# One PSUM tile of eight banks, and one reader instruction for both heads' scores

## The chip, the cores and the metric

The kernel runs on one NeuronCore of a Trainium2 chip. Its engines work side by side, each through its own list of instructions in order: TensorE (PE in the profile, with its weight loads as PEld), VectorE (DVE), ScalarE (ACT), GpSimd (POOL) and SyncE (SP, which here issues most of the DMAs). They wait for one another by semaphores. Matrix products go into PSUM, a memory of eight banks; a bank holds 512 fp32 numbers for each of 128 partitions, which is one score block here. VectorE and ScalarE read the results from there.

The metric is the time of one execution on the device in microseconds (us); less is better.

## The reference, cut to what matters

The model mixes a self-attention of 32 heads with a channel MLP, token by token, by a gate. All data are fp32.

```
B, S, D = 1, 2048, 576;  H = 32;  Dh = D // H = 18;  F = 4608
g = sigmoid((x * gate_w).sum(-1, keepdims=True))

q, k, v = split(x @ wqkv)                         # 32 heads of 18
scores = einsum("bhqd,bhkd->bhqk", q, k) * Dh ** -0.5
p = softmax(scores, axis=-1)
a = einsum("bhqk,bhkd->bhqd", p, v) -> (S, D) @ wo

y = layernorm(x)
h = gelu(y @ w1 + b1)                             # tanh form
b = h @ w2 + b2
out = g * a + (1 - g) * b
```

## The kernel before

**Attention.** The heads are taken in 16 pairs, and the 2,048 queries in two halves, which makes 32 units. TensorE has 128 rows; head 0 of a pair stands in rows 0 to 63 and head 1 in rows 64 to 127, so that the two heads' score products of L230 or L275, which use 54 to 56 rows each, can run at the same time. The softmax needs each query's largest score before the exponentials, and the kernel computes the scores twice for that:

- *Maxima rounds* (`s1_round`, L220): 128 queries against 512 keys. For each head one matmul (L230) writes a PSUM bank, and one VectorE `tensor_reduce` (L232) reads it and writes the 128 maxima of that block into `M4`. A unit has 32 rounds, there are 1,024 in all. They run ahead of the unit that uses them. When a unit is complete, `s1_finish` (L234) makes the maxima into two extra rows of the query operand.
- *Exponential rounds* (`s2`, L267): 128 keys against 512 queries, with the maxima subtracted by the extra rows. For each head one matmul (L275) writes a bank and one ScalarE `activation` with Exp (L278) reads it into a tile `p`, which has room for both heads. These, too, are 1,024 rounds.
- *Products with V* (`pv`, L282): matmuls of L293 multiply `p` by V, into one accumulator bank for a unit (16 chunks of 128 keys), which `o_store` (L300) copies out and sends to DRAM. They come in groups, 16 matmuls for two chunks or 24 for three.

**The MLP as filler.** The MLP's work is cut into small pieces by a generator (`mlp`, L342) and put between the rounds. Its first product, `h_pair` (L465, matmuls of L494), writes two banks for two chunks of the hidden layer, 54 matmuls for a pair; VectorE and ScalarE read these (L514, L515), and the GELU goes on over ScalarE and GpSimd. Its second product, `out_pair` (L552, matmuls of L582), writes two banks too, 48 matmuls for 128 tokens, and VectorE adds them to a running sum (L599). Before the attention loop stands the phase that makes Q, K and V (L886 to L918, with transposes and layer norm), with some maxima rounds between; after it the product with `wo` (`out_proj`, L1041, L1229).

**The order.** The kernel sets `manual_schedule`, so that each engine executes in the order in which the program calls it; the framework adds the semaphores. In the loop at L1280 each step is a key chunk of a unit: an exponential round, filler, a maxima round, at every second or third step a group of L293, then again an exponential round, filler, a maxima round, filler. The lengths of filler pieces and the due times of deferred work (`defer`, `run_due`) are written in as estimated nanoseconds.

**PSUM banks before.** Each use has its own pool of one-bank tiles: `ps_s1` (three banks) and `ps_o` (one) throughout, `ps_a` (four) before the loop, and in its place `ps_s2` (two) and `ps_w` (two) in the loop. `score_bank` (L121) gives a score matmul its bank. It is called once for each head, and counts through five banks in the loop (three of `ps_s1`, two of `ps_s2`) and four before it (three of `ps_s1`, and `ps_o`). A matmul that is to write a bank waits until the last reader of what stood in it is done.

Of the kernel before, what the change touches and what calls it, by code (L numbers as in the profile page):

```python
# [8 lines left out]
F32 = mybir.dt.float32  # L9
F32R = mybir.dt.float32r  # L10
AF = mybir.ActivationFunctionType
ALU = mybir.AluOpType
# [4 lines left out]
P = 128  # L17
# [16 lines left out]
GC0 = 1.0 / 0.044715  # L34
LN_EPS = 1e-5
HALF = S // 2
NS1 = 3
LEAD = 4
FILL = 1250.0
SLOT = 950.0  # L40
# [29 lines left out]
def gated_mix_kernel(ctx: ExitStack, tc: tile.TileContext, x, wqkv, wo, w1, b1, w2, b2, gate_w, out):  # L70
# [32 lines left out]
    pp = ctx.enter_context(tc.tile_pool(name="pp", bufs=2))  # L103
    hp = ctx.enter_context(tc.tile_pool(name="hp", bufs=6))
    asm = ctx.enter_context(tc.tile_pool(name="asm", bufs=2))
    ps_s1 = ctx.enter_context(tc.tile_pool(name="ps_s1", bufs=NS1, space=PSUM))
    ps_o = ctx.enter_context(tc.tile_pool(name="ps_o", bufs=1, space=PSUM))
    QA = [att.tile([P, HALF], F32R, name=f"qa{i}") for i in range(3)]
    KA = [att.tile([P, S], F32R, name=f"ka{i}") for i in range(2)]
    VT = [att.tile([P, NT, VW], F32, name=f"vt{i}") for i in range(2)]  # L110
# [2 lines left out]
    V0 = att.tile([P, NT, VW], F32, name="v0")  # L113
    oe = att.tile([P, TB], F32, name="oe")

    def psum(pool):
        return pool.tile([P, TB], F32, name="ps")

    ring = [0]

    def score_bank():  # L121

        ring[0] += 1
        if not looped[0]:
            return psum(ps_s1 if ring[0] % (NS1 + 1) < NS1 else ps_o)
        return psum(ps_s1 if ring[0] % (NS1 + 2) < NS1 else ps_s2)

    def big_tile():
        return yp.tile([P, 9, TB], F32R, name="big")
# [62 lines left out]
    def unit(u):  # L192
        return UNITS[u]
# [26 lines left out]
    def s1_round(u, r):  # L220


        t, kb = (r % 8, r // 8) if u in (0, NU - 3) else divmod(r, 4)
        if r == 0:
            M4[u] = asm.tile([P, 2, 8, 4], F32, name="m4")
        qa, ka = QA[u % 3], KA[unit(u)[0] % 2]
        for h in range(2):
            r0 = 64 * h
            ps = score_bank()
            nc.tensor.matmul(ps, qa[r0:r0 + 54, t * P:(t + 1) * P], ka[r0:r0 + 54, kb * TB:(kb + 1) * TB],  # L230
                             start=True, stop=True)
            nc.vector.tensor_reduce(M4[u][:, h, t, kb:kb + 1], ps, axis=AX.X, op=ALU.max)  # L232

    def s1_finish(u):  # L234

# [28 lines left out]
    def p_of(n):  # L264
        return RING[n % 4 if n < TWOS else (n - TWOS) % 3]

    def s2(u, kc, qb):  # L267
        qa, ka = QA[u % 3], KA[unit(u)[0] % 2]
        n = u * NT + kc
        if n < 2 and qb == 0:  # L270
            RING.insert(n, pp.tile([P, 2, 2, TB], F32, name="p"))
        ps = [score_bank() for _ in range(2)]
        for h in range(2):
            r0 = 64 * h
            nc.tensor.matmul(ps[h], ka[r0:r0 + 56, kc * P:(kc + 1) * P], qa[r0:r0 + 56, qb * TB:(qb + 1) * TB],  # L275
                             start=True, stop=True)
        for h in range(2):
            nc.scalar.activation(p_of(n)[:, qb, h], ps[h], AF.Exp, scale=SCALE)  # L278

    OB = {}  # L280

    def pv(n, m):  # L282

        u, kc = divmod(n, NT)
        if kc == 0:
            OB[u] = psum(ps_o)
        v = v_of(unit(u)[0])
        for c in range(n, n + m):
            for qb in range(2):
                for h in range(2):  # L290
                    r = 32 * (2 * h + qb)
                    k = c % NT
                    nc.tensor.matmul(OB[u][r:r + 32, :], v[:, k, 19 * h:19 * h + 32], p_of(c)[:, qb, h, :],  # L293
                                     start=(k == 0), stop=(k == NT - 1))
        if kc + m == NT:
            o_store(u, OB.pop(u))
# [45 lines left out]
    def mlp():  # L342
# [122 lines left out]
        def h_pair(q, last, inner=False):  # L465
# [5 lines left out]
                yield 0  # L471
            wt = ready(W1, q)
            del W1[q]
            ps = [psum(ps_w) for _ in range(2)]
            if q == 0:
                slots = [(w_, 0, c) for c in range(9) for w_ in (0, 1)] + [(0, 1, c) for c in range(9)]
            else:
# [74 lines left out]
        def out_pair(i, t, acc):  # L552

            tb, g = seq[i]
            tok = slice(t * P, (t + 1) * P)
            cs = [slice(nn * ND, (nn + 1) * ND) for nn in range(2)]
            ps = [psum(ps_w) for _ in range(2)]
            skip.clear()
            if piece[0]:
                ends = cuts(24, GAPS - piece[0]) | {12}  # L560
            elif rounds:
                ends = set(TURNS)
                skip.add(3)
            else:
                ends = set(TAIL)
                skip.update((2, 3))
            k = 0
            ends_at = []
            for turn in range(2):
                if turn == 1:  # L570
                    nc.tensor.wait_ge(swap, swaps[0])
                for j in ORDER:
                    while (i, j) not in HT:
                        cut[0] = 3
                        yield 0
                    hh, hl = HT[i, j]
                    w_ = ready(W2, (i * (G // 2) + j // 2, j % 2))
                    for h_, p_ in ((hh, 0), (hh, 1), (hl, 0)):
                        for h in (0, 1) if turn == 0 else (1, 0):
                            r = slice(64 * h, 64 * h + 64)  # L580
                            nn = h ^ turn
                            mm = nc.tensor.matmul(ps[nn][:, :ND], h_[r, tok], w_[p_][r, cs[nn]],  # L582
                                                  start=(k == 0), stop=(k == 6 * G - 1))
                            if k == 3 * G - 1:
                                ends_at.append(mm)
                        k += 1
                        if k == 3 * G:

                            seen = nc.scalar.sem_inc(swap, 1)
                            swaps[0] += 1  # L590
                            for mm in ends_at:
                                behind_of(seen, mm)
                        if k < 6 * G:
                            if k in ends:
                                cut[0] = 1
                            yield 131
            for nn in range(2):
                dst = acc[:, t, cs[nn]]
                nc.vector.scalar_tensor_tensor(dst, ps[nn][:, :ND], 0.5, b2b[:, cs[nn]] if g == 0 else dst,  # L599
                                               op0=ALU.mult, op1=ALU.add)  # L600
            if g == NG - 1:
                tt = tb * 4 + t
                nc.gpsimd.tensor_scalar(acc[:, t, :], acc[:, t, :], gate1[:, tt:tt + 1], 1.0, op0=ALU.mult, op1=ALU.mult)

                def store():
                    nc.sync.dma_start(b_scr[tt * P:(tt + 1) * P, :], acc[:, t, :])
                    kept[0] += 1
                defer(12 if tb < NB - 1 else 4, store)
            cut[0] = 2
            yield 131  # L610
# [106 lines left out]
    with ExitStack() as a:  # L717
        wpool = a.enter_context(tc.tile_pool(name="a_w", bufs=1, side="right"))
        sm = a.enter_context(tc.tile_pool(name="a_sm", bufs=2, side="right"))
        ps_a = a.enter_context(tc.tile_pool(name="ps_a", bufs=4, space=PSUM))  # L720

        qkstack = ExitStack()
        wqk = qkstack.enter_context(tc.tile_pool(name="a_wqk", bufs=1))
# [41 lines left out]
                eng.tensor_tensor(lo[:, cs], raw[:, cs], hi[:, cs].bitcast(F32), op=ALU.subtract)  # L765

        def transposed(tb, c):
            ps = psum(ps_a)
            for t in range(4):
                nc.tensor.transpose(ps[:, t * P:(t + 1) * P], x_view(tb)[:, t, c * P:(c + 1) * P], ident)  # L770
            return ps
# [63 lines left out]

        def stat_rows(tb):

            ps = psum(ps_a)
            nc.tensor.transpose(ps[:, :P], stp, ident)
            nc.scalar.activation(strow, ps[:8, :P], AF.Copy)  # L840
            nc.sync.dma_start(st_scr[tb], strow)
# [44 lines left out]
        def qk_group(tb, mt):  # L886
            big = xT[tb]
            wh, wl = W_QK
            ms = slice(mt * P, (mt + 1) * P)
            ps = psum(ps_a)  # L890
            k = 0
            for c in range(4):
                for w_, s_ in ((wh, c), (wh, 4 + c), (wl, c)):
# [12 lines left out]
        def v_group(tb, t, n, between=None):  # L906
# [1 line left out]
            tok = slice(t * P, (t + 1) * P)  # L908
            cs = slice(n * ND, (n + 1) * ND)
            wh, wl = W_V  # L910
            ps = psum(ps_a)
            k = 0
            for c in range(4):
                for s_, w_ in ((c, wh), (c, wl), (4 + c, wh)):
# [36 lines left out]
        for tb in range(NB):  # L951
            work = [(qk_group, (tb, mt)) for mt in (range(9) if tb < 2 else (4, 0, 1, 2, 3, 5, 6, 7, 8))] + [(v_group, (tb, t, n)) for t in range(4) for n in range(2)]
            for g, (fn, args) in enumerate(work):
# [35 lines left out]
                if tb == NB - 1:  # L989
                    if g == 0:  # L990
                        next(stream[0])
                    if g == 1:
                        load_k(0, 3 * TB, S)
                    if g == 2:
                        load_q(1)
                        next(stream[0])
                    if g == 9:
                        qkstack.close()
                        wp1 = mstack.enter_context(tc.tile_pool(name="m_w1", bufs=3))
                        wp2 = mstack.enter_context(tc.tile_pool(name="m_w2", bufs=4))  # L1000
                        next(stream[0])
                    if g == 7:
                        ps = psum(ps_a)
                        nc.tensor.transpose(ps[:, :NFC], b1r, ident[:NFC, :NFC])
                        nc.vector.tensor_copy(b1t, ps[:, :NFC])
                if tb == 1 and g == 5:
# [19 lines left out]
                    run_due()  # L1026


    ps_s2 = ctx.enter_context(tc.tile_pool(name="ps_s2", bufs=2, space=PSUM))
    ps_w = ctx.enter_context(tc.tile_pool(name="ps_w", bufs=2, space=PSUM))  # L1030
    cw = ctx.enter_context(tc.tile_pool(name="c_w", bufs=1, side="right"))
    ring2 = cw.tile([P, 2, 2, TB], F32, name="ring2")
    rstack = ExitStack()
# [7 lines left out]
    def out_proj():  # L1041
# [165 lines left out]
        for b in range(NB):  # L1207
# [6 lines left out]
            for t in range(4):  # L1214
# [5 lines left out]
                res = io.tile([P, D], F32, name="res", bufs=6)  # L1220
                for n in range(2):
                    cs = slice(n * ND, (n + 1) * ND)
                    ps = psum(ps_w)
                    k = 0
                    for c in range(5):
                        while done[b] <= c:
# [120 lines left out]
```

## Time and profile before

| | |
|---|---|
| time, median of 3 runs | 2213.79 us (2212.21 to 2215.25) |
| the profiled execution | 2212.78 us |
| its span, first to last instruction | 2211.0 us |
| TensorE busy | 2197.4 us, 99% of the span |
| VectorE busy | 1647.9 us, 75% |
| ScalarE busy | 1425.9 us, 64% |
| GpSimd busy | 1003.7 us, 45% |
| L232, maxima | 2,048 instructions, 684 ns each |
| L278, exponentials | 2,048 instructions, 596 to 597 ns each |

How to read the rows that follow. A group of instructions is told as line, engine, operation, output<-input, and shapes; behind the count (x) stand the busy time in us and the mean of one in ns, and behind the bar the engine's idle time just before these instructions, with whom it waited for. In a row of the timeline the first number is the start in us from the span's beginning, the second the length, and the last number behind an x how many instructions in a row are merged; [0.30 <-ACT p L278] says that the engine had been idle for 0.30 us and that this instruction released it. In a row of the busy time by stage the stage and its length come first, then busy us and count for PE, PEld, DVE, ACT and POOL (or for PE and PEld alone, where a single line's instructions are asked for), the granted TensorE clock (1.00 is full), the share of the DMA engines and GB/s. Matmuls overlap in TensorE's pipeline, so that their lengths add up to more than the time that they take.

### The profile page before, as it was taken

The page shows a single profiled execution, that of the slowest core. Times are in us where ns is not written, and L with a number is a line of the kernel's source. Part 1 is how long each engine was busy: PE and PEld are TensorE (multiplying, and loading weights), DVE is VectorE, ACT ScalarE, POOL GpSimd, SP SyncE. Part 2 cuts the span into 40 slices and gives each one's busy share as a digit, 9 for nine tenths or more (in the row PEclk, how much of TensorE's full clock was granted, in tenths as well). Part 3 has the DMA queues.
Part 4 walks back from the last instruction along what each step waited for, and adds up shares of the span by engine and source line. Part 5 has one row for each costly group of instructions (what it writes and reads, how often), then busy time and mean ns, then how long its engine had stood idle before and what let it go on. Part 6 is the DMA issues. An engine that isn't in the chain of part 4 may idle for free.

```text
span 2211.0 us, 51479 instructions
## 1 busy us (share of the span) xinstructions
PE 2197.4 (99%) x20496; PEld 1578.5 (71%) x20496; DVE 1647.9 (75%) x2888; ACT 1425.9 (64%) x2623; POOL 1003.7 (45%) x1000
## 2 busy tenths in 40 slices
PE   8999999999999999999999999999999999999999
PEld 7877666676667776677766777767776777776668
DVE  6675777777778778777777777777776777777734
ACT  4333777777776666666666666666665666666672
POOL 4331766666664444444444444444444444444800
PEclk9999999999999999999999999999999999999999
DMA  8867655444464623333354424233464333242265
GB/s 263 276 217 224 199 175 156 154 160 151 152 198 139 197 101 123 121 124 105 115 173 150 138 81 136 101 125 101 125 176 146 109 113 120 98 153 101 77 224 169
DMA packets 171640, 329.74 MB, mean 149 GB/s; under 512 B 65314, under 2 KB 91614, under 8 KB 160672
## 3 DMA queue, kind: packets, MB, share of 16 engines
q1 hardware_dynamic: 168850, 322.67, 45.2%
q8 instruction: 161, 2.64, 0.5%
q10 hardware_dynamic: 2454, 3.75, 0.5%
q14 instruction: 79, 0.65, 0.1%
q0 software_dynamic: 96, 0.03, 0.0%
HBM read 234.00 MB, written 96.69 MB: 150 GB/s over the span
## 4 chain that ended last, share of the span: by engine, by line
PE 95%; DVE 2%; DMA 1%; issue 0%; POOL 0%; ACT 0%; SPq 0%; DVEq 0%; ACTq 0%; POOLq 0%
PE ps L293 21%; PE ps L582 21%; PE ps L494 20%; PE ps L275 13%; PE ps L230 11%; PE ps L894 3%; PE ps L1229 3%; PE ps L915 2%; DVE m L232 1%; PE ps L770 0%; DMA p<-in_A_wqkv_dram 0%; DMA big<-y_scr 0%; PE ps L897 0%; PE ps L896 0%; DVE st L857 0%
## 5 line engine op out<-in xcount | busy, mean ns | idle before, releaser
L232 DVE TENSOR_REDUCE m<-ps 128x1 f32<-128x512 f32 x2048 | 1311.3, 684 | 390.3 <-PE ps L230 380.3
L278 ACT ACTIVATE p<-ps 128x512 f32<-128x512 f32 x1048 | 568.3, 597 | 301.7 <-PE ps L275 299.3
L278 ACT ACTIVATE ring<-ps 128x512 f32<-128x512 f32 x1000 | 543.2, 596 | 294.9 <-PE ps L275 291.8
L494 PE MATMUL ps<-big,w 64*128 64x512 f32 x3708 | 569.4, 393 | 0.2 <-issue 0.2
L183 POOL TENSOR_SCALAR zz<-zz 128x512 f32<-128x512 f32 x288 | 178.1, 618 | 743.3 <-ACT zz L547 686.1
L582 PE MATMUL ps<-w,hh 64*128 64x288 f32 x4352 | 477.4, 294 | 1.5 <-DVE x L599 1.5
L275 PE MATMUL ps<-qa,ka 56*128 56x512 f32 x2048 | 448.6, 420 | 1.1 <-ACT p L278 0.3
L582 PEld LDWEIGHTS ps<-w,hh 64*128 64x128 f32 x4352 | 417.2, 186 | 32.5 <-DVE x L599 6.2
L230 PE MATMUL ps<-ka,qa 54*128 54x512 f32 x2048 | 425.6, 397 | 0.1
L494 PEld LDWEIGHTS ps<-big,w 64*128 64x128 f32 x3708 | 369.8, 187 | 66.1 <-issue 0.5
L183 POOL TENSOR_TENSOR zz<-zz,z 128x512 f32<-128x512 f32 x288 | 371.4, 1290 | 24.0
L275 PEld LDWEIGHTS ps<-qa,ka 56*128 56x128 f32 x2048 | 204.4, 184 | 226.3 <-DVE m L232 174.7
L582 PE MATMUL ps<-w,hl 64*128 64x288 f32 x2176 | 339.3, 292 | 0.8 <-POOL hl L183 0.8
L293 PE MATMUL ps<-p,vt 128*32 128x512 f32 x1968 | 239.1, 598 | 0.0
L230 PEld LDWEIGHTS ps<-ka,qa 54*128 54x128 f32 x2048 | 213.4, 184 | 22.6 <-DVE m L232 2.6
L293 PE MATMUL ps<-ring,vt 128*32 128x512 f32 x1872 | 227.6, 598 | 0.0
L582 PEld LDWEIGHTS ps<-w,hl 64*128 64x128 f32 x2176 | 222.2, 184 | 1.2 <-POOL hl L183 1.1
L183 POOL TENSOR_TENSOR hl<-zz,hh 128x512 fp32r<-128x512 f32 x136 | 176.6, 1299 | 11.4
L183 POOL TENSOR_TENSOR w<-x,w 128x576 fp32r<-128x576 f32 (+1 forms) x54 | 98.8, 1842 | 164.1 <-ACT w L398 158.4
L293 PEld LDWEIGHTS ps<-p,vt 128*32 128x32 f32 x1968 | 52.5, 109 | 111.8 <-issue 102.7
L293 PEld LDWEIGHTS ps<-ring,vt 128*32 128x32 f32 x1872 | 49.8, 109 | 106.4 <-issue 106.4
L599 DVE SCALAR_TENSOR_TENSOR x<-ps,x 128x288 f32<-128x288 f32 x256 | 103.6, 446 | 8.8 <-PE ps L582 8.4
(121 smaller groups left out, 1538.2 us busy)
## 6 DMA issues: line engine op xcount, KB each, us to landing
w<-w_scr SPq DMA_DIRECT2D x54, 1152.0 KB
w<-w_scr SPq DMA_DIRECT2D x108, 576.0 KB
x<-in_B_w_dram SPq DMA_DIRECT2D x72, 288.0 KB
w_scr<-w SPq DMA_DIRECT2D x18, 1152.0 KB
w_scr<-w SPq DMA_DIRECT2D x36, 576.0 KB
qa<-qk_scr SPq DMA_DIRECT2D x192, 72.0 KB
ka<-qk_scr SPq DMA_DIRECT2D x84, 144.0 KB
qk_scr<-hh SPq DMA_DIRECT2D x36, 256.0 KB
```

The source lines that it names most:

```text
L183: fn(*args, **kw)
L230: nc.tensor.matmul(ps, qa[r0:r0 + 54, t * P:(t + 1) * P], ka[r0:r0 + 54, kb * TB:(kb + 1) * TB], start=True, stop=True)
L232: nc.vector.tensor_reduce(M4[u][:, h, t, kb:kb + 1], ps, axis=AX.X, op=ALU.max)
L275: nc.tensor.matmul(ps[h], ka[r0:r0 + 56, kc * P:(kc + 1) * P], qa[r0:r0 + 56, qb * TB:(qb + 1) * TB], start=True, stop=True)
L278: nc.scalar.activation(p_of(n)[:, qb, h], ps[h], AF.Exp, scale=SCALE)
L293: nc.tensor.matmul(OB[u][r:r + 32, :], v[:, k, 19 * h:19 * h + 32], p_of(c)[:, qb, h, :], start=(k == 0), stop=(k == NT - 1))
L494: nc.tensor.matmul(ps[h], wt[w_][r, c, :], y[r, c, :], start=(k == 0), stop=(k == 26))
L582: mm = nc.tensor.matmul(ps[nn][:, :ND], h_[r, tok], w_[p_][r, cs[nn]], start=(k == 0), stop=(k == 6 * G - 1))
L599: nc.vector.scalar_tensor_tensor(dst, ps[nn][:, :ND], 0.5, b2b[:, cs[nn]] if g == 0 else dst, op0=ALU.mult, op1=ALU.add)
L894: nc.tensor.matmul(ps, w_[:, c, ms], big[:, s_, :], start=(k == 0), stop=False)
L915: nc.tensor.matmul(ps[:, :ND], big[:, s_, tok], w_[:, c, cs], start=(k == 0), stop=False)
L1229: nc.tensor.matmul(ps[:, :ND], OT[b][2][:, s_, tok], w_part(w_, c)[:, cs], start=(k == 0), stop=(k == 13))
```

## The change: one tile, one reader for two heads

All eight banks become a single tile `PS` of 128 x 8 x 512. The pools are replaced by a table of bank numbers for each use, dealt out in turn: `"a"` before the loop, `"o"` for the accumulator of L293, `"w"` for the MLP and the output product, `"s"` for scores (banks 0, 1, 2, 5 before the loop and 0 to 4 in it). A score round takes its two banks at once with `score_banks`, as one operand over both: the two bank numbers in rising order, with the step between them. The matmuls still write one bank each. Then one VectorE instruction takes the maxima of both heads, and one ScalarE instruction the exponentials of both. Everything else is called in the same order as before.

```
-    def psum(pool):
-        return pool.tile([P, TB], F32, name="ps")
-    ring = [0]
-    def score_bank():
-        ring[0] += 1
-        if not looped[0]:
-            return psum(ps_s1 if ring[0] % (NS1 + 1) < NS1 else ps_o)
-        return psum(ps_s1 if ring[0] % (NS1 + 2) < NS1 else ps_s2)
+    PS = ctx.enter_context(tc.tile_pool(name="ps", bufs=1, space=PSUM)).tile([P, 8, TB], F32, name="ps")
+    BANKS = {"s": (0, 1, 2, 5), "a": (3, 4, 6, 7), "o": (5,), "w": (6, 7)}
+    given = {}
+    def bank(use):
+        given[use] = given.get(use, -1) + 1
+        return BANKS[use][given[use] % len(BANKS[use])]
+    def psum(use):
+        return PS[:, bank(use)]
+    def score_banks():
+        lo, hi = sorted((bank("s"), bank("s")))
+        return PS[:, lo:hi + 1:hi - lo]
...
+        ps = score_banks()
         for h in range(2):
             r0 = 64 * h
-            ps = score_bank()
-            nc.tensor.matmul(ps, qa[r0:r0 + 54, t * P:(t + 1) * P], ka[r0:r0 + 54, kb * TB:(kb + 1) * TB],
+            nc.tensor.matmul(ps[:, h], qa[r0:r0 + 54, t * P:(t + 1) * P], ka[r0:r0 + 54, kb * TB:(kb + 1) * TB],
                              start=True, stop=True)
-            nc.vector.tensor_reduce(M4[u][:, h, t, kb:kb + 1], ps, axis=AX.X, op=ALU.max)
+        nc.vector.tensor_reduce(M4[u][:, :, t, kb], ps, axis=AX.X, op=ALU.max)
...
-        ps = [score_bank() for _ in range(2)]
+        ps = score_banks()
         for h in range(2):
             r0 = 64 * h
-            nc.tensor.matmul(ps[h], ka[r0:r0 + 56, kc * P:(kc + 1) * P], qa[r0:r0 + 56, qb * TB:(qb + 1) * TB],
+            nc.tensor.matmul(ps[:, h], ka[r0:r0 + 56, kc * P:(kc + 1) * P], qa[r0:r0 + 56, qb * TB:(qb + 1) * TB],
                              start=True, stop=True)
-        for h in range(2):
-            nc.scalar.activation(p_of(n)[:, qb, h], ps[h], AF.Exp, scale=SCALE)
+        nc.scalar.activation(p_of(n)[:, qb], ps, AF.Exp, scale=SCALE)
...
-    ps_s2 = ctx.enter_context(tc.tile_pool(name="ps_s2", bufs=2, space=PSUM))
-    ps_w = ctx.enter_context(tc.tile_pool(name="ps_w", bufs=2, space=PSUM))
+    BANKS["s"] = (0, 1, 2, 3, 4)
+    given["s"] = -1
```

In the other places `psum(ps_a)`, `psum(ps_o)` and `psum(ps_w)` become `psum("a")`, `psum("o")` and `psum("w")`.

More of the change, by code (lines that the diff above doesn't have):

```diff
@@ L36 @@
 HALF = S // 2
-NS1 = 3
 LEAD = 4
@@ L105, in gated_mix_kernel @@
     asm = ctx.enter_context(tc.tile_pool(name="asm", bufs=2))
-    ps_s1 = ctx.enter_context(tc.tile_pool(name="ps_s1", bufs=NS1, space=PSUM))
-    ps_o = ctx.enter_context(tc.tile_pool(name="ps_o", bufs=1, space=PSUM))
+    PS = ctx.enter_context(tc.tile_pool(name="ps", bufs=1, space=PSUM)).tile([P, 8, TB], F32, name="ps")
     QA = [att.tile([P, HALF], F32R, name=f"qa{i}") for i in range(3)]
@@ L285, in pv @@
         if kc == 0:
-            OB[u] = psum(ps_o)
+            OB[u] = psum("o")
         v = v_of(unit(u)[0])
@@ L473, in h_pair @@
             del W1[q]
-            ps = [psum(ps_w) for _ in range(2)]
+            ps = [psum("w") for _ in range(2)]
             if q == 0:
@@ L556, in out_pair @@
             cs = [slice(nn * ND, (nn + 1) * ND) for nn in range(2)]
-            ps = [psum(ps_w) for _ in range(2)]
+            ps = [psum("w") for _ in range(2)]
             skip.clear()
@@ L719, in gated_mix_kernel @@
         sm = a.enter_context(tc.tile_pool(name="a_sm", bufs=2, side="right"))
-        ps_a = a.enter_context(tc.tile_pool(name="ps_a", bufs=4, space=PSUM))
         qkstack = ExitStack()
@@ L767, in transposed @@
         def transposed(tb, c):
-            ps = psum(ps_a)
+            ps = psum("a")
             for t in range(4):
@@ L836, in stat_rows @@
         def stat_rows(tb):
-            ps = psum(ps_a)
+            ps = psum("a")
             nc.tensor.transpose(ps[:, :P], stp, ident)
@@ L889, in qk_group @@
             ms = slice(mt * P, (mt + 1) * P)
-            ps = psum(ps_a)
+            ps = psum("a")
             k = 0
@@ L910, in v_group @@
             wh, wl = W_V
-            ps = psum(ps_a)
+            ps = psum("a")
             k = 0
@@ L1002, in gated_mix_kernel @@
                     if g == 7:
-                        ps = psum(ps_a)
+                        ps = psum("a")
                         nc.tensor.transpose(ps[:, :NFC], b1r, ident[:NFC, :NFC])
@@ L1222, in out_proj @@
                     cs = slice(n * ND, (n + 1) * ND)
-                    ps = psum(ps_w)
+                    ps = psum("w")
                     k = 0
```

## Prediction

> **What bounds the kernel now.** I read the page's head, its busy times, its chain of work and its groups first.
>
> ```profile
> span 2211.0 us, 51479 instructions
> ...
> PE 2197.4 (99%) x20496; PEld 1578.5 (71%) x20496; DVE 1647.9 (75%) x2888; ACT 1425.9 (64%) x2623; POOL 1003.7 (45%) x1000
> ...
> PE 95%; DVE 2%; DMA 1%; issue 0%; POOL 0%; ACT 0%; SPq 0%; DVEq 0%; ACTq 0%; POOLq 0%
> PE ps L293 21%; PE ps L582 21%; PE ps L494 20%; PE ps L275 13%; PE ps L230 11%; PE ps L894 3%; PE ps L1229 3%; PE ps L915 2%; DVE m L232 1%; PE ps L770 0%; DMA p<-in_A_wqkv_dram 0%; DMA big<-y_scr 0%; PE ps L897 0%; PE ps L896 0%; DVE st L857 0%
> ...
> L232 DVE TENSOR_REDUCE m<-ps 128x1 f32<-128x512 f32 x2048 | 1311.3, 684 | 390.3 <-PE ps L230 380.3
> L278 ACT ACTIVATE p<-ps 128x512 f32<-128x512 f32 x1048 | 568.3, 597 | 301.7 <-PE ps L275 299.3
> ```
>
> TensorE is the bound: 99% busy, 95% of the chain, and its order is written out by hand, so an instruction of it that waits holds up all behind it. The two engines that read the scores have idle time, 390.3 us ahead of the maxima alone, nearly all of it waiting for TensorE. So a microsecond saved on them is worth about nothing, and one microsecond of new waiting on TensorE is one microsecond of run time. What I had to find out is whether TensorE gets such waits.
>
> The second view is the busy time by stage; the row to read is the attention loop, up to the last maxima.
>
> ```profile
> 0.00:50.00 50.00, 44.41 (x221) 37.45 (x222) 31.74 (x75) 21.65 (x35) 20.62 (x24) 1.00 0.89 264
> 227.00:2096.00 1869.00, 1866.09 (x18370) 1310.11 (x18364) 1444.65 (x2487) 1285.74 (x2364) 924.08 (x931) 1.00 0.42 135
> ```
>
> TensorE (first number after the length) is busy for 1866.09 of 1869.00 us: there is no hole in which a new wait could vanish.
>
> **The change, part by part.** Call the two score matmuls of L230 with their maxima a maxima round, and the two of L275 with their exponentials an exponential round. They alternate strictly in the loop.
>
> *Readers.* Two instructions of 512 columns become one of 1,024. Nothing in the trace reads two banks, so I take the fixed part once and the slope from the same engines' longer and shorter instructions.
>
> ```profile
> L398 ACT ACTIVATE w<-x 128x576 fp32r<-128x576 f32 x36 | 23.9, 690 | 0.1
> ...
> L398 ACT ACTIVATE w<-x 128x1152 fp32r<-128x1152 f32 x18 | 21.0, 1165 | 0.0
> ...
> L239 DVE TENSOR_REDUCE nm<-m 128x16 f32<-128x64 f32 x32 | 7.0, 220 | 1.1
> ```
>
> ScalarE: (1165 - 690) / 576 = 0.825 ns a column, so 597 + 512 x 0.825 = 1.02 us. VectorE: (684 - 220) / (512 - 64) = 1.036 ns, so 684 + 512 x 1.036 = 1.22 us. Bounds: below, the columns with no fixed part, 0.85 and 1.06 us; above, what today's pair takes from start to end, 1.09 and 1.29 us (rows further down). I take 1.02 and 1.22, since each has one fixed part like any row here. The gain per round is then 0.07 us on an engine that waits anyway: no term of the sum.
>
> *Banks.* This is the part that counts. Today the loop deals out five score banks singly, one per head. A head's matmul therefore waits for the read of five heads earlier: the first head for the second read of three rounds back, the second head for the **first** of the two reads of two rounds back, which is the previous round of its own kind. After the change five banks are dealt out in twos: (0,1), (2,3), (4,0), (1,2), (3,4), and again. Go through them: each pair holds exactly one bank of the pair two rounds earlier, and its reader now gives back both banks together, at the end. So every round waits for the **whole** read of the previous round of its own kind: a maxima round for 1.22 us of VectorE where 0.68 us were enough, an exponential round for 1.02 us of ScalarE where 0.60 were. Five banks in twos are only two pairs deep.
>
> What such a wait looks like, and what a return costs, the trace shows at one place where ScalarE was late. First TensorE, then ScalarE:
>
> ```profile
> 674.20 0.39 PE L275 MATMUL ps<-qa,ka 56*128 56x512 f32 x1
> 674.89 0.49 PE L275 MATMUL ps<-qa,ka 56*128 56x512 f32 x1 [0.30 <-ACT p L278]
> ```
>
> ```profile
> 674.24 1.57 ACT L278 ACTIVATE p<-ps 128x512 f32<-128x512 f32 x3
> ```
>
> The first exponential ends at 674.24 + 0.60 = 674.84; the second head's matmul starts 0.05 us later and takes 0.49 instead of 0.39, since its weights are no longer loaded ahead. From return to matmul I charge 0.05 + 0.10 = 0.15 us; bounds 0.05 (the filling is hidden) and 0.18.
>
> *Where it bites.* Now a stretch between two groups of L293, filled with the MLP's second matmul (L582). TensorE's rows, then ScalarE's first exponential, then VectorE:
>
> ```profile
> 1003.99 0.41 PE L230 MATMUL ps<-ka,qa 54*128 54x512 f32 x2
> ...
> 1004.61 0.41 PE L275 MATMUL ps<-qa,ka 56*128 56x512 f32 x2
> ...
> 1005.64 0.42 PE L230 MATMUL ps<-ka,qa 54*128 54x512 f32 x2
> 1005.89 0.41 PE L275 MATMUL ps<-qa,ka 56*128 56x512 f32 x2
> ...
> 1006.92 0.41 PE L230 MATMUL ps<-ka,qa 54*128 54x512 f32 x2
> ...
> 1007.56 0.40 PE L275 MATMUL ps<-qa,ka 56*128 56x512 f32 x2
> ...
> 1008.19 0.41 PE L230 MATMUL ps<-ka,qa 54*128 54x512 f32 x2
> ```
>
> ```profile
> 1003.78 1.09 ACT L278 ACTIVATE p<-ps 128x512 f32<-128x512 f32 x2 [0.59 <-PE ps L275]
> ```
>
> ```profile
> 1004.42 1.29 DVE L232 TENSOR_REDUCE m<-ps 128x1 f32<-128x512 f32 x2 [1.22 <-PE ps L230]
> 1006.08 2.56 DVE L232 TENSOR_REDUCE m<-ps 128x1 f32<-128x512 f32 x4 [0.38 <-PE ps L230]
> ```
>
> The four maxima of 1006.08 run to 1008.64, and the third of them, whose bank is wanted next, to about 1008.0; the maxima round of 1008.19 starts before the fourth is done. Today's order only just fits. A reader starts 0.43 us after its matmuls (1003.99 to 1004.42); I use that for both engines. With the new waits, and each delay passed on to all that follows:
>
> - second exponential round: bank back at 1003.78 + 1.02, so not before 1004.95; its own time 1004.61. Wait 0.34.
> - second maxima round: 1004.42 + 1.22 + 0.15 = 1005.79, own 1005.98. None.
> - third exponential round: 1004.95 + 0.43 + 1.02 + 0.15 = 1006.55, own 1006.23. Wait 0.32.
> - third maxima round: 1005.98 + 0.43 + 1.22 + 0.15 = 1007.78, own 1007.58. Wait 0.20.
> - fourth maxima round: 1007.78 + 1.80 = 1009.58, own 1008.19 + 0.86 = 1009.05. Wait 0.53.
>
> Sum 1.39 us. The fourth exponential round gets no wait (limit 1006.55 + 1.60 = 1008.15, own 1007.56 + 0.86). Behind each wait stand TensorE's MLP matmuls and the next L293; VectorE, ScalarE and the stores behind them only come later by as much. The group of L293 behind them gives both readers time, so the next stretch begins afresh. How many such stretches there are: the L582 matmuls of this one and of the whole loop,
>
> ```profile
> 1003.20:1008.60 5.40, 4.22 (x48) 3.96 (x48) 1.00 0.73 251
> ```
>
> ```profile
> 227.00:2096.00 1869.00, 599.42 (x6708) 557.94 (x6710) 1.00 0.42 135
> ```
>
> so 6708 / 48 = 140, and 140 x 1.39 = 195 us. The rest of the loop is filled with the MLP's first matmul (L494), 72 pairs of chunks by the program's loops (4 blocks, 9 groups, 2 pairs). L230 in such a stretch:
>
> ```profile
> 1456.99 0.40 PE L230 MATMUL ps<-ka,qa 54*128 54x512 f32 x2
> ...
> 1458.62 0.40 PE L230 MATMUL ps<-ka,qa 54*128 54x512 f32 x2
> ```
>
> ```profile
> 1454.50:1463.80 9.30, 2.30 (x12) 1.13 (x12) 1.00 0.76 252
> ```
>
> Six rounds, so five gaps, of 1.63 us where 0.43 + 1.22 + 0.15 = 1.80 are needed: 5 x 0.17 = 0.85 us, for 72 pairs (an estimate: some of them have more room, some less) 61 us.
>
> *The rest.* Which bank numbers the accumulators use is renaming. Before the loop the maxima rounds have four banks in twos and stand among long projections; after 2096 there are no maxima left. I charge nothing for either; their cover is the work of L894 and L293 between two rounds. Nothing is moved on any DMA queue, and TensorE waits on fewer semaphores, which I also count as nothing, as the chain has 0% of issue.
>
> *Sum.* 195 + 61 = 256 us, on the profiled execution's own 2212.8 us (span 2211.0): **2469 us**, 11.6% more. The median shown is 1 us above that execution. With the lower bounds the first kind of stretch loses 0.60 us and the second nothing: 84 us, 2297. With the upper ones 1.69 and 1.35: 334 us, 2547.
>
> **The rivals.**
>
> *One read in the time of one head (faster).* If an instruction took two banks side by side, at 0.60 and 0.68 us, banks would come back as soon as now and the engines would be freed of half their reading. It decides from a pair's read of about 0.7 us downwards, at the shortest gap of 1.27 us (1006.92 to 1008.19) less 0.43 and 0.15. Against it: every row of L398 and L239 grows with its columns. Its gain is capped by VectorE's maxima on the chain, 1% of the span: 2212.8 - 22 = 2191 us. In the Trainium skill, VectorE: DVE Perf Modes, section "The perf-mode tier table", tensor_reduce runs at one element a cycle from any memory, which speaks against it. The same page's rules advise fewer instructions, because of the fixed cost of each; the row of L239 agrees that there is one, but no engine that it would relieve bounds this kernel.
>
> *Half of the wait is hidden.* Only one head of a round waits for the round before last; the other's banks are back, and the two heads stand in different halves of TensorE's rows. If the half that doesn't wait runs on while the other stands, half the sum is lost: 2212.8 + 128 = 2341 us. For it: the two matmuls at 674 start apart. Against: the second one there left TensorE idle for 0.30 us, and what follows in program order uses both halves.
>
> *The pair counts as all that lies between.* The third pair, banks 4 and 0, is one strided operand. If its waits are kept for the whole stretch of banks 0 to 4, the two rounds behind each such pair wait for its reader too: the next round is due about 0.65 us later (half of 1.27) and gets 0.43 + 1.02 + 0.15 = 1.60 us or more, so some 1.0 us for each of 2048 / 5 = 410 rounds, less what the main case already takes there (about 0.25 each, 100 us): 2469 + 310 = 2780 us. The change would then not do what it says, to deal out banks. Nothing in this trace bears on it.
>
> *TensorE's clock falls.* New idle time of 256 in 2469 us is 10%. If the clock then fell to 0.9 in the loop, its 1866 us would take 207 more: 2676 us. Against it: in the first 50 us TensorE is idle for 11%, at a granted clock of 1.00. The Trainium skill, TensorE: Matmul & The Clock Gate, section "A second HAM failure mode: psum-queue depth-cycling", says that short idles between groups while cycling through PSUM banks make the clock swing between half and full; that first row doesn't agree.
>
> **How the numbers follow.** What this measurement can tell from no change is about 0.2%, 4 us. Chances: bank return as worked out 0.77 (its own range 2297 to 2547); half hidden 0.10; strided pair 0.04; clock 0.03; faster 0.04; no difference, because the waits fall into room that I don't see, 0.02. So faster 0.04, same 0.02, slower 0.94. The range 2300 to 2560 holds the first two cases and leaves out what is beyond.
>
> **What would show it.** L232 and L278 should stand with 1,024 instructions each (1,024 exponentials over both destinations), at about 1220 and 1020 ns. L230's and L275's matmuls and weight loads should show idle time released by L232 and L278, some 256 us in all; TensorE's busy share should fall to about 90%, and the chain should pass through VectorE and ScalarE, with maxima rounds no closer than 1.80 us in the stretches of L582. I am wrong if a pair's read is far from 1.02 and 1.22 us, if rounds follow one another in less than a read plus 0.5 us, or if TensorE stays at 99%.

## The result, and the profile after

| | time, median (lowest to highest) | ratio to the kernel before, 95% interval |
|---|---|---|
| before | 2213.57 us (2212.09 to 2215.25) | |
| changed | 2927.57 us (2914.11 to 2932.50) | 1.322 [1.319, 1.325] |

The changed kernel is slower by 714 us, 32%. The forecast was slower by 256 us, 2469 us, with 2560 us as the upper end: the right side, and far too little. The profiled execution took 2932.5 us.

First the changed kernel's page: busy times, chain, and the groups that the change touches. L232 and L277 are now the score matmuls of maxima and exponential rounds, L234 and L279 their readers.

```profile
PE 2490.7 (85%) x20496; PEld 1619.3 (55%) x20496; DVE 1595.3 (54%) x1864; ACT 1369.2 (47%) x1599; POOL 1001.5 (34%) x1000
...
PE 63%; DVE 18%; ACT 11%; issue 2%; DMA 1%; SPq 0%; DVEq 0%; ACTq 0%
...
L234 DVE TENSOR_REDUCE m<-ps 128x2 f32<-128x1024 f32 x1024 | 1251.9, 1224 | 1054.9 <-PE ps L232 878.2
L279 ACT ACTIVATE p<-ps 128x1024 f32<-128x1024 f32 x524 | 536.5, 1025 | 675.3 <-PE ps L277 567.9
...
L232 PE MATMUL ps<-ka,qa 54*128 54x512 f32 x2048 | 545.5, 440 | 215.6 <-ACT p L279 98.9
L277 PE MATMUL ps<-qa,ka 56*128 56x512 f32 x2048 | 538.2, 453 | 180.9 <-DVE m L234 170.4
```

Two things stand as forecast: half as many readers, of 1224 and 1025 ns (1220 and 1020 were expected), and a chain that passes through VectorE (18%) and ScalarE (11%), where it was TensorE to 95%. The last two rows were not expected. TensorE's maxima matmuls wait for **ScalarE's exponentials**, and its exponential matmuls for **VectorE's maxima**: each for the reader of the other kind of round, which no bank shared two rounds back explains. The list of waits has more of it, between the readers themselves:

```profile
PE ps L277 <- DVE m L234: 170.4, 155, 1.5
...
PE ps L232 <- ACT p L279: 98.9, 99, 1.7
PE ps L232 <- ACT ring L279: 92.3, 98, 1.7
DVE m L234 <- ACT ring L279: 85.1, 60, 3.9
DVE m L234 <- ACT p L279: 70.3, 55, 3.8
ACT p L279 <- DVE m L234: 62.3, 50, 2.8
ACT ring L279 <- DVE m L234: 52.6, 42, 1.6
```

Columns: total us, times, the longest. On TensorE 170.4 + 98.9 + 92.3 = 362 us are idle for the other kind's reader, and 270 us of idle time of the two readers ended only with the other reader's instruction, though the two share nothing but PSUM. (That is all of the idle time before these instructions; a part of it the reader would have stood idle anyway.) One place in the timeline of the changed kernel, TensorE, then ScalarE, then VectorE:

```profile
1404.92 0.50 PE L277 MATMUL ps<-qa,ka 56*128 56x512 f32 x2
...
1407.46 0.50 PE L232 MATMUL ps<-ka,qa 54*128 54x512 f32 x2 [1.58 <-ACT p L279]
```

```profile
1406.39 1.02 ACT L279 ACTIVATE p<-ps 128x1024 f32<-128x1024 f32 x1 [2.82 <-DVE m L234]
```

```profile
1405.08 1.22 DVE L234 TENSOR_REDUCE m<-ps 128x2 f32<-128x1024 f32 x1
```

The exponential round of 1404.92 has the strided pair, banks 4 and 0. Its matmuls were done by about 1405.4. ScalarE could have begun then; it begins at 1406.39, when the maxima of the round before end (1405.08 + 1.22 = 1406.30). The next maxima matmuls begin 0.05 us after that exponential ends (1406.39 + 1.02 = 1407.41), though it is not their bank that it gives back. Three rounds stand in one line.

### The profile page after: what moved, and what is told of

The parts are those of the page before. It is cut to its first block, busy times and chain, and to the rows that moved or that the text cites. A ratio compares the mean times of both kernels' runs of the same rounds, so it can differ in the third digit from the quotient of the medians.

```text
span 2930.7 us, 50161 instructions
## 1 busy us (share of the span) xinstructions
PE 2490.7 (85%) x20496; PEld 1619.3 (55%) x20496; DVE 1595.3 (54%) x1864; ACT 1369.2 (47%) x1599; POOL 1001.5 (34%) x1000
## 4 chain that ended last, share of the span: by engine, by line
PE 63%; DVE 18%; ACT 11%; issue 2%; DMA 1%; SPq 0%; DVEq 0%; ACTq 0%
DVE m L234 17%; PE ps L294 17%; PE ps L232 12%; PE ps L277 11%; PE ps L495 11%; PE ps L583 8%; ACT ring L279 5%; ACT p L279 5%; PE ps L894 2%; PE ps L1229 1%; PE ps L915 1%; DMA bt<-b_scr 0%; DMA out_dram<-res 0%; DVE x L600 0%; ACT hh L900 0%
## 5 line engine op out<-in xcount | busy, mean ns | idle before, releaser
L234 DVE TENSOR_REDUCE m<-ps 128x2 f32<-128x1024 f32 x1024 | 1251.9, 1224 | 1054.9 <-PE ps L232 878.2
L279 ACT ACTIVATE p<-ps 128x1024 f32<-128x1024 f32 x524 | 536.5, 1025 | 675.3 <-PE ps L277 567.9
L279 ACT ACTIVATE ring<-ps 128x1024 f32<-128x1024 f32 x500 | 512.5, 1025 | 654.5 <-PE ps L277 553.4
L232 PE MATMUL ps<-ka,qa 54*128 54x512 f32 x2048 | 545.5, 440 | 215.6 <-ACT p L279 98.9
L277 PE MATMUL ps<-qa,ka 56*128 56x512 f32 x2048 | 538.2, 453 | 180.9 <-DVE m L234 170.4
L277 PEld LDWEIGHTS ps<-qa,ka 56*128 56x128 f32 x2048 | 242.8, 185 | 516.7 <-DVE m L234 256.5
L583 PE MATMUL ps<-w,hh 64*128 64x288 f32 x4352 | 524.3, 298 | 0.6 <-DVE x L600 0.6
L232 PEld LDWEIGHTS ps<-ka,qa 54*128 54x128 f32 x2048 | 248.1, 185 | 386.2 <-ACT p L279 130.4
L583 PE MATMUL ps<-w,hl 64*128 64x288 f32 x2176 | 381.3, 293 | 0.0
L583 PEld LDWEIGHTS ps<-w,hl 64*128 64x128 f32 x2176 | 262.2, 186 | 0.2
L294 PE MATMUL ps<-p,vt 128*32 128x512 f32 x1968 | 247.4, 614 | 0.0
L294 PE MATMUL ps<-ring,vt 128*32 128x512 f32 x1872 | 239.3, 625 | 0.0
L894 PE MATMUL ps<-big,wqk 128*128 128x512 f32 x432 | 117.3, 423 | 16.0 <-DVE m L234 15.0
L294 PEld LDWEIGHTS ps<-p,vt 128*32 128x32 f32 x1968 | 53.3, 111 | 113.0 <-issue 111.9
```

Source lines behind the costliest of these rows:

```text
L232: nc.tensor.matmul(ps[:, h], qa[r0:r0 + 54, t * P:(t + 1) * P], ka[r0:r0 + 54, kb * TB:(kb + 1) * TB], start=True, stop=True)
L234: nc.vector.tensor_reduce(M4[u][:, :, t, kb], ps, axis=AX.X, op=ALU.max)
L277: nc.tensor.matmul(ps[:, h], ka[r0:r0 + 56, kc * P:(kc + 1) * P], qa[r0:r0 + 56, qb * TB:(qb + 1) * TB], start=True, stop=True)
L279: nc.scalar.activation(p_of(n)[:, qb], ps, AF.Exp, scale=SCALE)
L894: nc.tensor.matmul(ps, w_[:, c, ms], big[:, s_, :], start=(k == 0), stop=False)
```

## The experiments

Two theories. *Bank return*, the prediction's: every round waits for the whole read of the last round of its own kind, since five banks in twos are two pairs deep. *Strided stretch*, a rival there with a chance of 0.04: the operand over banks 0 and 4 is kept as if it took banks 0 to 4, so that whatever uses a bank between them waits for its reader too. Comparisons are with runs of the kernel before on the same chip, 2212.3 to 2212.4 us.

### Adjacent pairs alone

```
-    BANKS = {"s": (0, 1, 2, 5), "a": (3, 4, 6, 7), "o": (5,), "w": (6, 7)}
+    BANKS = {"s": (0, 1, 2, 3), "a": (4, 5, 6, 7), "o": (5,), "w": (6, 7)}
...
-    BANKS["s"] = (0, 1, 2, 3, 4)
+    BANKS["s"] = (0, 1, 2, 3)
```

> The changed kernel, with four score banks in place of five, dealt out as (0,1), (2,3) and again; before the loop the same four, with 4 to 7 for the projections. No pair is strided any more. Bank return alone (every round waits for the whole read of the last round of its own kind; two pairs deep, as five banks in twos are): the 2469 us of the prediction, between 2300 and 2550. If waits kept for all banks between a strided pair's two cost the rest, this run stands some 460 us under the changed kernel's 2928. If reading 1,024 columns at once is what costs, it stays near 2928.

Measured: 2488.28 us, ratio 1.125 [1.123, 1.126], 276 us more than the kernel before. With **one bank less** it is 439 us faster than the changed kernel. Its waits on TensorE for score readers:

```profile
PE ps L232 <- DVE m L234: 42.3, 151, 0.5
...
PE ps L277 <- ACT p L279: 6.5, 34, 0.4
PE ps L277 <- ACT ring L279: 6.1, 32, 0.6
```

Each kind waits for its own kind only, and no reader waits for the other. One stretch between two groups of L294, TensorE, then VectorE:

```profile
1140.88 0.50 PE L277 MATMUL ps<-qa,ka 56*128 56x512 f32 x2
...
1145.40 0.50 PE L232 MATMUL ps<-ka,qa 54*128 54x512 f32 x2
...
1147.22 0.50 PE L232 MATMUL ps<-ka,qa 54*128 54x512 f32 x2 [0.28 <-DVE m L234]
...
1149.51 0.50 PE L277 MATMUL ps<-qa,ka 56*128 56x512 f32 x2
```

```profile
1145.94 1.23 DVE L234 TENSOR_REDUCE m<-ps 128x2 f32<-128x1024 f32 x1 [0.59 <-PE ps L232]
```

The maxima rounds stand 1.82 us apart. The read ends at 1147.17, and 0.05 us later the next one's matmuls begin and take 0.50 instead of 0.40. The stretch takes 1149.51 - 1140.88 = 8.63 us. The one that the prediction went through took 7.14 in the kernel before, from its first row to

```profile
1003.25 0.51 PE L275 MATMUL ps<-qa,ka 56*128 56x512 f32 x2
...
1010.39 0.49 PE L275 MATMUL ps<-qa,ka 56*128 56x512 f32 x2
```

so 1.49 us more, where 1.39 were worked out. This is the forecast's mechanism, and close to its size: 276 us against 256.

### The same four banks, strided

```
-    BANKS["s"] = (0, 1, 2, 3)
+    BANKS["s"] = (0, 2, 1, 3)
```

> The same four banks, dealt out as (0,2), (1,3): as deep as the run beside it, and every pair strided. If waits are kept bank by bank: the same time as with adjacent pairs. If they are kept for the whole stretch between a pair's two banks, the pairs overlap in banks 1 and 2, and every round waits for the reader of the round just before it: 0.43 + 1.02 + 0.15 = 1.60 us after an exponential round and 1.80 after a maxima round, where the rounds of the kernel before come about 0.65 us apart in the stretches of L582. Seven such gaps a stretch make it some 6.7 us longer, and 250 stretches 1670 us: about 3900 us.

Measured: 4378.41 us in a single execution, at a mean granted clock of 0.79. Nothing differs from the run before but which two of four banks make a pair. In the loop the exponential rounds get banks 0 and 2, the maxima rounds 1 and 3. TensorE, ScalarE, VectorE:

```profile
2001.45 0.50 PE L232 MATMUL ps<-ka,qa 54*128 54x512 f32 x2 [0.42 <-ACT p L279]
...
2002.25 0.40 PE L277 MATMUL ps<-qa,ka 56*128 56x512 f32 x1
2003.34 0.49 PE L277 MATMUL ps<-qa,ka 56*128 56x512 f32 x1 [0.70 <-DVE m L234]
...
2004.95 0.50 PE L232 MATMUL ps<-ka,qa 54*128 54x512 f32 x2 [0.42 <-ACT p L279]
```

```profile
2003.87 1.02 ACT L279 ACTIVATE p<-ps 128x1024 f32<-128x1024 f32 x1 [1.95 <-PE ps L277]
```

```profile
2002.06 1.23 DVE L234 TENSOR_REDUCE m<-ps 128x2 f32<-128x1024 f32 x1 [2.27 <-PE ps L232]
```

Maxima matmuls at 2001.45, their read until 2003.29, the second exponential matmul at 2003.34, their read until 2004.89, maxima matmuls at 2004.95: one read after the other, 3.50 us for a pair of rounds against the 3.40 expected. Only the first exponential matmul goes ahead, at 2002.25, in the middle of the maxima's read. It writes bank 0, which lies outside the stretch from 1 to 3; the second writes bank 2, which the maxima's operand steps over, and waits for its reader. No maxima matmul goes ahead: the first of them writes bank 1, inside the stretch from 0 to 2. The strided stretch is shown, down to its two ends. The time above the expected 3900 us was not taken apart; the lower clock, of which more below, is likely a part of it.

### The changed kernel, its strided pairs read singly

```
-        nc.scalar.activation(p_of(n)[:, qb], ps, AF.Exp, scale=SCALE)
+        if adjacent[0]:
+            nc.scalar.activation(p_of(n)[:, qb], ps, AF.Exp, scale=SCALE)
+        else:
+            for h in range(2):
+                nc.scalar.activation(p_of(n)[:, qb, h], ps[:, h], AF.Exp, scale=SCALE)
```

and the same for the maxima.

> The changed kernel with its five banks and its deal, but the pairs that aren't adjacent, (4,0) in the loop and (2,5) before it, are read by two instructions, one for each bank, as in the kernel before; the adjacent pairs by one. Bank return alone still holds for it: 2400 to 2480 us, the lower part because every fifth round gives its banks back one by one. Strided stretch: it falls by the same 460 us as with adjacent pairs. If the depth of the deal counted for nothing, it would come to about 2213.

Measured: 2506.76 us, ratio 1.133 [1.131, 1.135]. 421 us of the changed kernel's loss go when no instruction reads an operand over two separate banks; the matmuls still write the same banks, so it is the reader's operand that counts. TensorE's largest wait for a reader is again for one of its own kind:

```profile
PE ps L234 <- DVE m L237: 43.4, 142, 0.4
```

The rest is put down to bank return, and the fifth bank bought nothing: it is 18 us slower than with four. The two readers still end 62 us of each other's idle time, against 270; why, the runs don't show.

### One tile, single reads

```
-        return PS[:, lo:hi + 1:hi - lo]
+        return [psum("s") for _ in range(2)]
```

with a reader for each bank, as before.

> The one tile of eight banks and its tables of bank numbers, but every bank read by an instruction of its own, as before. Both theories: no difference from the kernel before, 2213 us within 0.3%. If the single tile itself adds waits (its uses tied to one another), it is slower.

Measured: 2212.10 us, ratio 1.000 [0.999, 1.001]. That all banks are one tile costs nothing.

### Four banks, single reads

The tile and tables of the adjacent pairs, with the single reads of the run before.

> Four score banks dealt out singly, every bank read by an instruction of its own: the depth of the pairs without the pairs. If the depth of the deal is what costs, it is as slow as the adjacent pairs or a little slower, since a head now waits for the same head's read of two rounds back, the second head for the end of today's pair, 1.09 or 1.29 us instead of 1.02 or 1.22. By the prediction's schedule that is 1.60 us in a stretch of L582 and 1.28 in one of L494: 140 x 1.60 + 72 x 1.28 = 316, 2528 us. If it is the single read of both heads that costs, it comes to 2213 us.

Measured: 2370.41 us, ratio 1.071 [1.069, 1.073]: half of the 316 us expected. So less depth alone costs 158 us, and reading both heads at once 118 more. The schedule treats a round's two heads as one, and one place shows what that leaves out. TensorE and VectorE:

```profile
1014.81 0.39 PE L231 MATMUL ps<-ka,qa 54*128 54x512 f32 x1
1014.97 0.39 PE L231 MATMUL ps<-ka,qa 54*128 54x512 f32 x1
```

```profile
1015.24 2.03 DVE L233 TENSOR_REDUCE m<-ps 128x1 f32<-128x512 f32 x3 [0.62 <-PE ps L231]
```

The second head waited and came 0.16 us after the first; VectorE began 0.43 us after the **first**. With single reads the reader works on one head while the other's matmul still waits, so that a delay isn't handed on whole. One reader for both starts after the later of the two. That this accounts for the whole of the missing half is argued from such places, not measured.

### One kind in pairs

```
+    BANKS["e"] = (0, 1)
+    BANKS["s"] = (2, 3, 4)
```

In the loop one kind is read in pairs from banks 0 and 1, the other singly from 2, 3 and 4. First the exponentials in pairs, then the maxima.

> Only the exponentials are read in pairs, always from banks 0 and 1; the maxima singly, in turn from banks 2, 3 and 4. An exponential round still waits for the whole read of the one before it (1.02 us), a maxima round only for the first head's read (0.68). Bank return by the prediction's schedule: 0.66 us in a stretch of L582 and 0.24 in one of L494: 110 us, 2322 us. If the loss were shared by the instruction count or came from anything that both kinds have in common, about half of the adjacent pairs' 276 us: 2350 us.

> The reverse: only the maxima are read in pairs, from banks 0 and 1 in the loop, the exponentials singly from 2, 3 and 4. A maxima round waits for 1.22 us of the one before it, an exponential round for 0.60. By the same schedule 1.20 us in a stretch of L582 and 0.84 in one of L494: 228 us, 2441 us, which together with the pair of the exponentials is more than both at once, since a round that one wait has delayed needs less of the other. A rule of halves gives 2350 us.

Measured: 2375.53 us, ratio 1.074 [1.072, 1.075], and 2470.62 us, ratio 1.116 [1.115, 1.118]. That is 163 us where 110 were expected, and 258 where 228 were. The two are unequal and add up to 421, more than the 276 of both at once, as the schedule has it; halves are ruled out. In the run with the exponentials in pairs some 24 us of the loss arise where no maxima rounds are left: from the last maxima matmul to the last product with V it takes 91.2 us, against 66.8 in the kernel before. Every exponential round there waits for the one just before it, on the only pair. In the other run the same stretch takes 85.5 us, 19 more, with the exponentials singly on three banks. The schedule had left both out; without them the two runs lose some 139 and 240 us.

### Half the columns

```
-        nc.vector.tensor_reduce(M4[u][:, :, t, kb], ps, axis=AX.X, op=ALU.max)
+        nc.vector.tensor_reduce(M4[u][:, :, t, kb], ps[:, :, 0:256], axis=AX.X, op=ALU.max)
```

on the adjacent pairs.

> The four adjacent banks, both kinds in pairs, but the maxima are taken over the first 256 of each head's 512 columns, so that the pair is read as fast as one head before (about 684 ns); the other half of the keys is left out of the maxima. The banks, the deal, the waits and the instruction counts are those of the adjacent pairs. If the length of the read is what TensorE waits for, the maxima rounds' waits vanish, and the exponentials' remain: 110 us, 2322 us against 2488. If it were the tie of two banks itself, it stays near 2488.

Measured: 2352.05 us, ratio 1.063 [1.061, 1.065], 136 us faster than the full read, where 166 were expected. The groups of this run:

```profile
L234 DVE TENSOR_REDUCE m<-ps 128x2 f32<-128x512 f32 x1024 | 705.9, 691 | 992.5 <-PE ps L232 992.3
...
L232 PE MATMUL ps<-ka,qa 54*128 54x512 f32 x2048 | 412.1, 398 | 0.0
```

The maxima matmuls have no idle time left, and are back at 398 ns. Still two banks, still one instruction: what TensorE waits for is the length of the read. The 140 us that remain are those of the exponentials' pair, as in the run above without its end (139), where the schedule had 110.

### The share before the loop

Only the first of the two table edits above: adjacent pairs before the loop, the changed kernel's five banks in it.

> The changed kernel with its five banks and strided third pair in the loop, but before the loop the four adjacent banks 0 to 3, and 4 to 7 for the projections. The strided pair (2,5) before the loop spans the projections' banks 3 and 4; the changed kernel reaches its first L294 at 273.7 us, the kernel before its own at 225.9. If that stretch causes it, this run reaches it at about 226 and is 48 us faster than the changed kernel, 2880 us; all else of the loss stays in the loop. If the delay has another cause, 2928 us.

Measured: 2881.09 us, ratio 1.301 [1.299, 1.304], 46 us faster than the changed kernel's median, and its first L294 comes at 228.2 us, not 273.7. In the changed kernel the pair (2,5) spans the projections' banks 3 and 4. The busy time of the stage from 60 us to the first L293 or L294, before and changed, and the changed kernel's wait there:

```profile
60.00:226.00 166.00, 165.73 (x921) 135.46 (x924) 114.39 (x224) 58.03 (x109) 45.62 (x33) 1.00 0.73 237
```

```profile
60.00:274.00 214.00, 180.52 (x927) 143.96 (x930) 113.45 (x181) 58.01 (x105) 46.32 (x33) 0.93 0.57 184
```

```profile
PE ps L894 <- DVE m L234: 15.0, 5, 3.1
```

The same work takes 214 us instead of 166 in the changed kernel, projections wait for maxima, and the clock is down to 0.93.

## Why the prediction was right in direction and wrong in size

The 714 us are, by the runs, about 276 of bank return with adjacent pairs (2488 against 2212), 393 of the strided pair in the loop (2881 against 2488), and 46 of the strided pair before it (2928 against 2881). Counted from the run that reads the strided pairs singly (2507), the first two are 294 and 374.

**The step that failed** is *Banks*: it deals out "(0,1), (2,3), (4,0), (1,2), (3,4)" and counts (4,0) as two banks like the others. Its one reader is held against all five banks, so that it waits for the reader before it, and the rounds behind it wait for it. That term is missing from the sum, and with its twin before the loop it is some 439 of the 714 us, more than the term that was worked out.

**Right.**
- *TensorE has no room.* No run with new waits on TensorE kept the old time.
- *Readers.* 1224 and 1025 ns for 1220 and 1020 (684 + 512 x 1.036 is 1.21 us, not 1.22; nothing hangs on it). No run gained by halving their number.
- *Two pairs deep, whole read.* Shown by the adjacent pairs (276 us for 256), by the fifth bank that buys nothing, and by the half read. That the size came out within 8% is in part luck: the same schedule gave 110 us where 139 and 140 were measured, 228 where it was 240, and 316 where it was 158.
- *0.15 us from return to matmul.* 0.05 and 0.10 in the row of 1147.22.

**Wrong.**
- *"Which bank numbers the accumulators use is renaming. Before the loop the maxima rounds have four banks in twos and stand among long projections ... I charge nothing."* The numbers decide what lies between a strided pair's two banks. It cost 46 us before the loop.
- *"Nothing in this trace bears on it"*, with 0.04 for the strided stretch. The trace could not decide it, and that was no ground for a low chance: the semaphores are the framework's, and how it keeps an operand with a step was not known. A rival that nothing speaks against belongs in the range. The mechanism was named there with its right place, each pair of banks 0 and 4.
- *Its price, 2780 us.* It gave 310 us to the strided pair in the loop, where the runs show 393 (or 374), and nothing to the one before it, 46. In the loop it left out that the strided pair's reader itself waits for the reader before it (the row of 1406.39), and the clock; how the difference is shared between the two wasn't measured.
- *"TensorE's clock falls"*, as a rival of its own with an average share of idle time against it. It came along with the stretch: a mean of 0.983, so (1 - 0.983) x 2930.7 / 0.5 = 100 us at half clock, since every drop in the trace is to 0.50; what they cost in time was not measured. The share of the first 50 us was the wrong measure (next section but one).
- *"TensorE's busy share should fall to about 90%"* as the sign of bank return. With adjacent pairs alone it shows 96% at 276 us more, in part since a matmul behind a wait is recorded as longer (446 ns for L232 on average against 397 in the kernel before), and with four banks read singly 99% at 158 us more. Nor do "some 256 us" of idle time stand before the matmuls: with adjacent pairs it is 55 us (42.3 + 6.5 + 6.1). The weight loads' share is the better sign: 71% before, 62% with adjacent pairs, 55% changed.

**Half right.** The rival *half of the wait is hidden* doesn't hold for pairs; for single reads from four banks its size does, 158 of 316 us.

What stays open: why the strided operand is kept for the whole stretch. The runs show that it is, for readers and writers on three engines; they don't show where in the framework. A form of the pair that avoids it, such as two tiles, wasn't tried. No run beat the kernel before.

## What to carry to other kernels

An instruction that reads two buffers gives both back at its end (here 118 us on top of the lost depth), so count how deep the ring is in the new units, and how long one unit is held, before counting the instructions saved; where the bound engine has no idle time, that delay is the price. An operand with a step over buffers may be tracked as everything in between: deal out neighbours, and look in the list of waits for engines that wait for readers whose buffer they don't use. A difference between two bank tables that changes nothing but adjacency separates the two in one run.

## What the runs showed of the hardware that was not expected

TensorE's clock falls for short stretches long before it is idle altogether. The busy time by stage of the changed kernel, in four stretches of 3.41 us one behind the other:

```profile
599.94:603.36 3.42, 2.16 (x22) 1.53 (x18) 1.61 (x3) 2.46 (x4) 1.46 (x2) 1.00 0.54 153
603.36:606.77 3.41, 3.41 (x17) 0.59 (x16) 1.72 (x3) 0.62 (x2) 3.16 (x5) 0.50 0.54 154
606.77:610.18 3.41, 2.05 (x22) 1.43 (x20) 1.23 (x1) 1.02 (x1) 2.93 (x3) 1.00 0.27 70
610.18:613.60 3.42, 3.42 (x41) 2.90 (x41) 1.38 (x2) 2.05 (x2) 0.00 (x0) 1.00 0.02 5
```

TensorE was busy for 2.16 of the first 3.42 us, its longest wait there being 1.11 us, and the stretch behind it ran at 0.50; then full speed again. The third stretch was busy for even less, 2.05 us, and the one behind it kept 1.00, so the busy share of one stretch doesn't settle it; what does stays open. With the reads in single file the mean over a run came to 0.79. The Trainium skill, TensorE: Matmul & The Clock Gate, section "Part 1: The HAM clock gate (the "warmup" mystery)", gives windows of 3.4 us and two states, full and half; the rows agree with both. The same page's section "A second HAM failure mode: psum-queue depth-cycling" warned of short idles between groups, and the prediction set the average of its first 50 us against it; the row at 0.50 agrees with the warning. An average over 50 us was no evidence against drops that last 3.41 us.
